# One fused kernel on one core: where the state's first expert products are kept between two steps, and when w2 is asked for

## The chip, the cores and the metric

The kernel runs on one core of a Trainium2 chip. The metric is device time in microseconds (us), as the median of several runs. TensorE (PE) does the matrix products, VectorE (DVE) and ScalarE (ACT) read its results out of PSUM, GpSimd (POOL) does some element-wise work, and SyncE (SP) issues most of the transfers (DMAs).

## The reference, cut to what matters

Three stages follow one another. `x` is (4, 8, 512, 64): 4 batches, 8 heads, 512 rows, 64 per head. `state` is (4, 8, 32, 64): 32 state slots per head.

```python
scores = scale * x @ state.T;   a  = softmax(scores);   xread = a @ state
scores2 = scale * state @ x.T;  a2 = softmax(scores2);  sread = a2 @ x
x1 = concat([xread, sread])                  # per batch 512 + 32 rows, 512 wide (8 heads x 64)
...
for e in range(8):                           # every token goes through every expert
    h = relu(x1 @ w1[e])                     # 512 -> 1024
    out += P[:, e:e + 1] * (h @ w2[e])       # 1024 -> 512
...
g = silu(out @ w_in); result = g @ w_out     # 512 -> 2048 -> 512
```

`P` is a softmax over the experts, balanced by 8 rounds of row and column sums. Since `xread = a @ state`, the product `xread @ w1[e]` equals `a @ (state @ w1[e])` head by head, and `state @ w1[e]` has only 32 rows per batch and head.

## The kernel before

All products are float32 made of three float32r products: each operand is split into a rounded high part and the rest, and `mm3` (L84 to L86) issues high x low, low x high, high x high. In this text `h_...` and `l_...` are the two parts of a weight, `hh` and `hl` those of the hidden values. `lo_of` (L89) writes a low part: source minus high part. The high part is a cast on ACT.

The second stage is bound to a list of steps. One expert is two **units** of 512 hidden columns, so there are 16 units `u`; a unit has 16 steps `k`, for batch b = k // 4 and hidden tile f = k % 4. Step i of the main loop issues on PE, in an order written out by hand: `S1` of the step two ahead (6 matmuls into `ph`, from the attention weights `aT` and `G[u, b]` = state @ w1), then `S2` of this step (12 matmuls into the four banks `po`, from `hh`, `hl` and the unit's w2), then small pieces. `S2`'s tile f of w2 is first needed at step k = f of its unit. ACT and DVE take `ph` to `hh` and `hl`. At the end of each batch four DVE operations add `po` to `acc` (L567). The order of the instructions on ACT, DVE, POOL and SP is made by a scheduler from the program's order; the order on PE is the program's.

`G` of unit u + 1 is made during unit u. `g_pair` is called inside `S2`, after its second tile, at steps 1 and 5 of most units (8 and 9 of unit 0, 8 and 10 of unit 1). It issues 12 products of half the contraction rows into four PSUM banks `pg`, two from the pool `p1` (2 banks, which `ph` uses too) and two from `pm` (2 banks, also for transposes and small results). For each bank ACT casts the high part, DVE makes the low part, both go into a tile `stg`, and a DMA writes it to DRAM (`g_d`). Four DMAs for each batch read it back (`load_g`, in the steps 8, 9, 11, 14), because a bank holds lanes (partitions) by batch and slot for one head, and `G` needs for one batch lanes by head and slot.

w1 and w2 come as raw tiles (`load_raw`, SP), which `load_split` casts on ACT and subtracts on DVE (on POOL in unit 0's w1). w2 of the next unit is asked for and cast at steps 12 to 15, behind `load_g` in the program, w1 of unit u + 2 at steps 7 to 10. At step 6 PE computes `psr` (the first product of the 32 x 4 `sread` rows; `sr_first`), and at step 7 `sread_second` adds their second product in a free `po` bank. The raw tiles share 3 buffers, the `stg` tiles 4.

Of the kernel before, what the change touches and what calls it, by code (L numbers as in the profile page):

```python
# [21 lines left out]
def fused_kernel(ctx: ExitStack, tc: tile.TileContext, x, state, w_gate, w1, w2, w_in, w_out, out):  # L22

# [79 lines left out]
    for b in range(B):  # L103
        nc.sync.dma_start(out=st[b * NS:(b + 1) * NS], in_=state[b].rearrange("h n d -> n h d"))
# [181 lines left out]
    def scores(b, rr, bank):  # L286
# [3 lines left out]
        for r in (2 * rr, 2 * rr + 1):  # L290
            for hp in range(KD):
# [3 lines left out]
                    bd[:, hp, bp, j ^ (hp & 1)].rearrange("p h n -> p (h n)"), start=True, stop=True,  # L295
# [33 lines left out]
    def positions(b, q):  # L329
# [4 lines left out]
        e2 = e2_of[b, q] = att.tile([128, 512], F32, tag="e2", name=f"e2_{b}_{q}", bufs=4)  # L334
# [91 lines left out]
    g_d = {}  # L426
# [4 lines left out]
    def g_pieces(u, hps, banks):  # L431
# [10 lines left out]
        for hp in hps:  # L442
            for half in range(2):
                ps = pg[hp, half]
                stg = stp.tile([128, 2, FU], F32R, tag="stg", name=f"stg{u}_{hp}_{half}")
                nc.scalar.copy(stg[:, 0], ps)
                lo_of(stg[:, 1], ps, stg[:, 0])
                nc.sync.dma_start(out=g_d[u][hp // 2, 2 * (hp & 1) + half], in_=stg.bitcast(F32))

    def g_first(bp, hp, bank=pm):  # L450
# [6 lines left out]
        halves = [(slice(64 * half, 64 * half + 64), 2 * bp + (half ^ (hp & 1))) for half in range(2)]  # L457
        for lanes, b in halves:
            nc.scalar.copy(G[0, b][lanes, hp // 2, 0], pg[lanes])
        for lanes, b in halves:  # L460
            lo_of(G[0, b][lanes, hp // 2, 1], pg[lanes], G[0, b][lanes, hp // 2, 0])

    def g_start(u):
        g_d[u] = dram.tile([2, 4, 128, 2, FU], F32, tag="g_d", name=f"g_d{u}", bufs=2)

    def g_pair(u, i):
        if i == 0:
            g_start(u)
        g_pieces(u, (2 * i, 2 * i + 1), (p1, pm))

    def load_g(u, b):
        g_tile(u, b)
# [5 lines left out]

    def sr_first(u):
# [22 lines left out]
    def S1(u, b, f):  # L502
# [11 lines left out]
        else:  # L514
# [88 lines left out]
    def both(piece, b, *bank):  # L603
# [165 lines left out]
```

## Time and profile before

| | |
|---|---|
| median of 3 runs | 1737.66 us (1737.47 to 1739.04) |
| profiled execution: its time, its span | 1744.39 us, 1742.6 us |
| TensorE's mean granted clock in it, share of full | 0.988 |
| PE, DVE, ACT, POOL busy in the span | 97%, 51%, 28%, 1% |
| DMA traffic in the span | 222.07 MB |

The span is the time from the first to the last instruction in the trace of one execution; its own time lies 6.7 us above the median of the runs, so a sum made on the span has to be set against that execution and then moved to the median. TensorE's share counts a matmul as busy from its start to its modelled end; neighbours overlap, so the start-to-start distance (0.227 us for a 512-column matmul at full clock) says more than the duration printed (0.39 us).

### The profile page before, as it was taken

To read this page: it belongs to the slowest core of one execution; us is meant where nothing else is said; L and a number is where in the kernel's file an instruction comes from. 1 tells how busy PE (TensorE), PEld (TensorE's weight loads), DVE (VectorE), ACT (ScalarE), POOL (GpSimd) and SP (SyncE) were. 2 spreads that over 40 slices of the span, in tenths; PEclk is the share of its full clock that TensorE was granted. 3 is DMA by queue.
4 is the path that set the end of the run, shared out by engine and by line. 5 is a ranking of instruction groups with operands and counts; after the bars stand their busy time and mean duration, and the time that the engine had idled before them with its cause. 6 is when DMAs were issued, how large, how long until landed. Compare 5 with 4: busy or idle time off the path is not lost.

```text
span 1742.6 us, 20238 instructions
## 1 busy us (share of the span) xinstructions
PE 1690.5 (97%) x7868; PEld 1396.2 (80%) x7868; DVE 891.2 (51%) x1524; ACT 492.3 (28%) x891; POOL 12.6 (1%) x15
## 2 busy tenths in 40 slices
PE   8999999999999999999999999999999999999999
PEld 7878787877878787878778787878788888888888
DVE  7642575555555555565655655465434433433333
ACT  5642244222222222232322222232212322222222
POOL 1010000000000000000000000000000000000000
PEclk9989999999999999999999999999999999999999
DMA  7042376565745464655647465655540103020211
GB/s 170 19 150 70 96 201 199 132 205 146 195 160 164 138 176 165 167 185 136 206 145 206 139 167 171 170 183 125 169 109 7 43 1 97 1 97 1 85 49 55
DMA packets 107631, 222.07 MB, mean 127 GB/s; under 512 B 28560, under 2 KB 44944, under 8 KB 107536
## 3 DMA queue, kind: packets, MB, share of 16 engines
q1 hardware_dynamic: 101152, 201.76, 40.5%
q10 hardware_dynamic: 6384, 19.02, 2.8%
q8 instruction: 62, 1.02, 0.2%
q14 instruction: 33, 0.27, 0.0%
HBM read 136.59 MB, written 84.15 MB: 127 GB/s over the span
## 4 chain that ended last, share of the span: by engine, by line
PE 79%; DVE 2%; issue 1%; ACT 1%; ACTq 0%; DVEq 0%
PE po L85 16%; PE po L84 15%; PE po L86 15%; PE ph L86 9%; PE ph L84 9%; PE ph L85 9%; PE pg L441 3%; DVE acc L567 1%; PE psr L85 1%; PE psr L84 1%; PE psr L86 1%; DVE l_w L89 1%; ACT hh L512 1%; PE px L591 0%; DVE hl L513 0%
## 5 line engine op out<-in xcount | busy, mean ns | idle before, releaser
L84 PE MATMUL po<-h_w,hl 128*128 128x512 f32 x1024 | 410.4, 401 | 22.7 <-ACT h_w L190 22.7
L85 PE MATMUL po<-l_w,hh 128*128 128x512 f32 x1024 | 406.6, 397 | 14.1 <-DVE l_w L89 14.1
L86 PE MATMUL po<-h_w,hh 128*128 128x512 f32 x1024 | 404.0, 395 | 0.0
L513 DVE SCALAR_TENSOR_TENSOR hl<-ph,hh 128x512 fp32r<-128x512 f32 x256 | 176.7, 690 | 419.8 <-ACT hh L512 419.3
L512 ACT ACTIVATE hh<-ph 128x512 fp32r<-128x512 f32 x256 | 153.2, 598 | 666.0 <-PE ph L86 662.2
L84 PEld LDWEIGHTS po<-h_w,hl 128*128 128x128 f32 x1024 | 194.7, 190 | 79.6 <-ACT h_w L190 29.8
L85 PEld LDWEIGHTS po<-l_w,hh 128*128 128x128 f32 x1024 | 195.0, 190 | 61.3 <-DVE l_w L89 22.5
L86 PEld LDWEIGHTS po<-h_w,hh 128*128 128x128 f32 x1024 | 195.1, 191 | 40.8
L84 PE MATMUL ph<-aTh,G 128*128 128x512 f32 x512 | 203.5, 398 | 0.4 <-DVE hl L513 0.4
L86 PE MATMUL ph<-aTh,G 128*128 128x512 f32 x512 | 200.2, 391 | 0.0
L85 PE MATMUL ph<-aTl,G 128*128 128x512 f32 x512 | 200.2, 391 | 0.0
L567 DVE SCALAR_TENSOR_TENSOR acc<-po,P,acc 128x512 f32<-128x512 f32 x224 | 153.1, 742 | 6.6 <-PE po L86 6.6
L523 DVE TENSOR_TENSOR gv<-ph,sg 128x384 f32<-128x384 f32 (+1 forms) x80 | 48.9, 611 | 191.2 <-ACT sg L521 191.2
L84 PE MATMUL ph<-x2h,wil 128*128 128x384 f32 (+1 forms) x320 | 115.4, 361 | 0.0
L86 PE MATMUL ph<-x2h,wih 128*128 128x384 f32 (+1 forms) x320 | 114.7, 358 | 0.0
L85 PE MATMUL ph<-x2l,wih 128*128 128x384 f32 (+1 forms) x320 | 114.4, 357 | 0.0
L86 PEld LDWEIGHTS ph<-aTh,G 128*128 128x128 f32 x512 | 96.5, 189 | 20.6
L84 PEld LDWEIGHTS ph<-aTh,G 128*128 128x128 f32 x512 | 96.9, 189 | 19.8 <-DVE hl L513 0.6
L85 PEld LDWEIGHTS ph<-aTl,G 128*128 128x128 f32 x512 | 96.8, 189 | 19.1
L86 PE MATMUL po<-woh,hh 128*128 128x512 f32 x272 | 106.8, 393 | 0.0
L85 PE MATMUL po<-wol,hh 128*128 128x512 f32 x272 | 106.7, 392 | 0.0
L84 PE MATMUL po<-woh,hl 128*128 128x512 f32 x272 | 105.8, 389 | 0.0
(163 smaller groups left out, 1848.9 us busy)
## 6 DMA issues: line engine op xcount, KB each, us to landing
g_d<-stg SPq DMA_DIRECT2D x120, 512.0 KB, 4.0
G<-g_d SPq DMA_DIRECT2D x240, 256.0 KB, 5.5
raw_w<-in_moe_w_dram SPq DMA_DIRECT2D x136, 256.0 KB, 5.3
raw<-in_moe_w_in_dram SPq DMA_DIRECT2D x16, 512.0 KB, 6.2
wi_d<-cvo ACTq DMA_DIRECT2D x16, 512.0 KB, 2.7
raw<-in_moe_w_out_dram SPq DMA_DIRECT2D x16, 512.0 KB, 6.3
wo_d<-cvo ACTq DMA_DIRECT2D x16, 512.0 KB, 3.1
x<-in_x_dram SPq DMA_DIRECT2D x16, 256.0 KB, 4.9
```

The costliest lines, as they stand in the source:

```text
L84: nc.tensor.matmul(ps, al, bh, start=first, stop=False)
L85: nc.tensor.matmul(ps, ah, bl, start=False, stop=False)
L86: nc.tensor.matmul(ps, ah, bh, start=False, stop=last)
L89: engine.tensor_tensor(out=lo, in0=src, in1=hi.bitcast(F32), op=ALU.subtract)
L441: nc.tensor.matmul(pg[hp, half], a[lanes[half], hp], w[lanes[half]], start=i == 0, stop=i == 2)
L512: nc.scalar.activation(out=hh, in_=ph, func=AF.Relu)
L513: last["dve"] = nc.vector.scalar_tensor_tensor(out=hl, in0=ph, scalar=0.0, in1=hh.bitcast(F32), op0=ALU.max, op1=ALU.subtract)
L523: nc.vector.tensor_tensor(out=gv[:, :n], in0=ph[:, :n], in1=sg[:, :n], op=ALU.mult)
L567: nc.vector.scalar_tensor_tensor(out=a, in0=ps, scalar=P[:, t, e:e + 1], in1=a, op0=ALU.mult, op1=ALU.add)
```

## The change

`state @ w1` no longer goes through DRAM. The (batch, head) pairs are placed so that every 32-lane quarter of a `pg` bank already stands on the lanes where its batch needs it (a Latin square over batch and head: `bd`, the attention scores' places and the reads of the slots follow the new placing). Each bank is copied, in float32, in four 32-lane pieces into one tile `g32`, two pieces by ACT and two by DVE in turn; `split_g` later makes the high part of one batch by an ACT cast of 128x1024 and the low part by a POOL subtraction, at steps 7, 8, 10, 14 (11 to 14 in units 0 and 1). `g_d` with its 360 transfers and the `stg` tiles go away. Raw w2 tiles are asked for at steps 10 (tile 0), 11 (tiles 1 and 2) and 12 (tile 3) for units from 1 on, with 4 raw buffers in place of 3; they are cast at steps 12 to 15 as before, now ahead of `split_g` in the program. At the start the state is loaded by eight transfers (four on SP, four on ACT) in place of four, its high and low part for `g_pair` are made by POOL from `bd`'s parts, the low parts of unit 1's w1 are also made on POOL, and `e2` has 3 buffers in place of 4. In step 2 of unit 0 `back(0)` stands ahead of `positions(1)`.

```diff
--- before
+++ after
...
     s8 = ctx.enter_context(tc.tile_pool(name="s8", bufs=8))
-    stp = ctx.enter_context(tc.tile_pool(name="stp", bufs=4))
+    gp = ctx.enter_context(tc.tile_pool(name="gp", bufs=1))
     accp = ctx.enter_context(tc.tile_pool(name="accp", bufs=4))
     wp = ctx.enter_context(tc.tile_pool(name="wp", bufs=5))
-    rawp = ctx.enter_context(tc.tile_pool(name="rawp", bufs=3))
+    rawp = ctx.enter_context(tc.tile_pool(name="rawp", bufs=4))
     hp_ = ctx.enter_context(tc.tile_pool(name="hp", bufs=4))
...
     st = att.tile([128, H, D], F32, tag="att", name="st")
-    for b in range(B):
-        nc.sync.dma_start(out=st[b * NS:(b + 1) * NS], in_=state[b].rearrange("h n d -> n h d"))
+    for p in range(2):
+        for b in range(B):
+            r, hs = NS * (b ^ p), slice(4 * p, 4 * p + 4)
+            (nc.scalar if p else nc.sync).dma_start(out=st[r:r + NS, hs], in_=state[b, hs].rearrange("h n d -> n h d"))
     x_sb = {}
...
     bd = const.tile([128, KD, 2, 2, 2, NS], F32, name="bd")
+    bdhl = gp.tile([128, 2, KD, 2, 2, 2, NS], F32R, tag="g32", name="bdhl")
+    bdh, bdl = bdhl[:, 0], bdhl[:, 1]
     sth = const.tile([128, KD, B * NS], F32R, name="sth")
...
         nc.tensor.transpose(pst4[:, hp].rearrange("p b n -> p (b n)"), st[:, 2 * hp:2 * hp + 2, :].rearrange("p h d -> p (h d)"), ident)
-    for hp in range(KD):
-        for j in range(2):
-            for half in range(2):
-                lanes = slice(64 * half, 64 * half + 64)
-                nc.vector.tensor_copy(
-                    bd[lanes, hp, :, j ^ (hp & 1), half, :],
-                    pst4[lanes, hp].rearrange("p (c j) n -> p c j n", j=2)[:, :, j, :],
-                )
+    for half in range(2):
+        lanes = slice(64 * half, 64 * half + 64)
+        for c in range(2):
+            nc.vector.tensor_copy(bd[lanes, :, c, :, half ^ c, :], pst4[lanes, :, 2 * c:2 * c + 2, :])
     flat = "p k c j h n -> p (k c j h n)"
-    bdh, bdl = (stp.tile([128, KD, 2, 2, 2, NS], F32R, tag="stg", name=f"bd{i}") for i in "hl")
     def split_state():
...
         lo_of(bdl.rearrange(flat), bd.rearrange(flat), bdh.rearrange(flat))
-        nc.scalar.copy(sth.rearrange("p k c -> p (k c)"), pst)
-        lo_of(stl.rearrange("p k c -> p (k c)"), pst, sth.rearrange("p k c -> p (k c)"))
+        for t, s in ((sth, bdh), (stl, bdl)):
+            v = s.bitcast(F32).rearrange("p k c j h n -> p k c (j h n)")
+            nc.gpsimd.tensor_tensor(out=t, in0=v[:, :, 0], in1=v[:, :, 1], op=ALU.add)
     def bd_of(t, hp, bp):
...
         else:
-            w1t[u, hp] = load_split(src, [128, FU], f"w1_{u}_{hp}", "w1", 4, nc.gpsimd if u == 0 else nc.vector)
-    def load_w2(u, f):
+            w1t[u, hp] = load_split(src, [128, FU], f"w1_{u}_{hp}", "w1", 4, nc.gpsimd if u <= 1 else nc.vector)
+    def load_w2(u, f, only_raw=False):
         e, fh = divmod(u, UPE)
         r0 = fh * FU + f * 128
-        w2t[u, f] = load_split(w2[e, r0:r0 + 128, :], [128, DM], f"w2_{u}_{f}", "w2", 5)
+        if only_raw:
+            load_raw(w2[e, r0:r0 + 128, :], [128, DM], f"w2_{u}_{f}")
+        else:
+            w2t[u, f] = load_split(w2[e, r0:r0 + 128, :], [128, DM], f"w2_{u}_{f}", "w2", 5)
...
             for half in range(2):
-                ps = pg[hp, half]
-                stg = stp.tile([128, 2, FU], F32R, tag="stg", name=f"stg{u}_{hp}_{half}")
-                nc.scalar.copy(stg[:, 0], ps)
-                lo_of(stg[:, 1], ps, stg[:, 0])
-                nc.sync.dma_start(out=g_d[u][hp // 2, 2 * (hp & 1) + half], in_=stg.bitcast(F32))
+                for i in range(4):
+                    to = (i // 2) ^ (hp // 2), half ^ (i & 1)
+                    r = slice(NS * i, NS * i + NS)
+                    dst = g32[u][r, 2 * to[1] + to[0], hp % 2]
+                    if i % 2 == half:
+                        nc.scalar.copy(dst, pg[hp, half][r])
+                    else:
+                        nc.vector.tensor_copy(dst, pg[hp, half][r])
     def g_first(bp, hp, bank=pm):
...
-    def g_start(u):
-        g_d[u] = dram.tile([2, 4, 128, 2, FU], F32, tag="g_d", name=f"g_d{u}", bufs=2)
+            lo_of(G[0, b][lanes, hp % 2, 1], pg[lanes], G[0, b][lanes, hp % 2, 0])
     def g_pair(u, i):
         if i == 0:
-            g_start(u)
+            g32[u] = gp.tile([128, B, 2, FU], F32, tag="g32", name=f"g32_{u}")
         g_pieces(u, (2 * i, 2 * i + 1), (p1, pm))
-    def load_g(u, b):
+    def split_g(u, b):
         g_tile(u, b)
-        for c in range(4):
-            r = NS * (c ^ (2 * (b & 1)))
-            nc.sync.dma_start(
-                out=G[u, b][r:r + NS].bitcast(F32), in_=g_d[u][:, c, b * NS:(b + 1) * NS].rearrange("q n w f -> n q w f")
-            )
+        src = g32[u][:, b]
+        nc.scalar.copy(G[u, b][:, :, 0], src)
+        lo_of(G[u, b][:, :, 1], src, G[u, b][:, :, 0], nc.gpsimd)
     def sr_first(u):
...
             mm3(ps, srh[:, hp], srl[:, hp], wh, wl, hp == 0, hp == KD - 1)
-        t = att.tile([128, FU], F32, tag="e2", name=f"hs_{u}", bufs=4)
+        t = att.tile([128, FU], F32, tag="e2", name=f"hs_{u}", bufs=3)
         nc.scalar.activation(out=t, in_=ps, func=AF.Relu)
...
         1: (both(positions, 0), [lambda hp=hp: x_turn(3, hp, pm) for hp in range(KD)]),
-        2: (both(positions, 1), both(back, 0) + both(scores, 3, pm) + [lambda: slots(3, 1), lambda: state_reads(0)]),
+        2: (both(back, 0), both(positions, 1) + both(scores, 3, pm) + [lambda: slots(3, 1), lambda: state_reads(0)]),
         3: (both(mixing, 2, pm), [lambda: g_first(1, 0)]),
...
                 convert_some((u - 2) * B * NF + k + 5)
+            if k >= 12:
+                load_w2(u + 1, k - 12) if u + 1 < NU else load_wout(0, k - 12)
             for unit, hp in first.get(u, {}).get(k, ()):
...
                 load_w1(u + 2, k - at)
-            loads = (12, 13, 14, 15) if u <= 1 else (8, 9, 11, 14)
+            for f in ({10: (0,), 11: (1, 2), 12: (3,)}.get(k, ()) if 1 <= u and u + 1 < NU else ()):
+                load_w2(u + 1, f, True)
+            loads = (11, 12, 13, 14) if u <= 1 else (7, 8, 10, 14)
             if u + 1 < NU and k in loads:
-                load_g(u + 1, loads.index(k))
-            if k >= 12:
-                load_w2(u + 1, k - 12) if u + 1 < NU else load_wout(0, k - 12)
+                split_g(u + 1, loads.index(k))
             if u == NU - 1:
```

How the change moves instructions, in unit 10 (in the names below the first number is the unit: `h_w2_10_2` is the high part of tile 2 of unit 10's w2, `stg11_0_1` the bank of head pair 0, half 1, of the next unit's G, `hh10_1_0` the hidden tile of batch 1, f = 0; the last number is a running one). On ACT before, around step 1 to 3:

```order
L512 ACTIVATE hh10_0_3_7333<-ph10_0_3_7326 128x512
L446 CAST stg11_0_0_7360<-pg11_0_0_7344 128x512
L446 CAST stg11_0_1_7364<-pg11_0_1_7345 128x512
L446 CAST stg11_1_0_7368<-pg11_1_0_7352 128x512
L446 CAST stg11_1_1_7372<-pg11_1_1_7353 128x512
L512 ACTIVATE hh10_1_0_7394<-ph10_1_0_7387 128x512
L190 CAST h_w2_10_2_7257<-raw_w2_10_2_7255 128x512
L190 CAST h_w2_10_3_7291<-raw_w2_10_3_7289 128x512
L512 ACTIVATE hh10_1_1_7418<-ph10_1_1_7411 128x512
```

The casts of w2's tiles 2 and 3 stand behind four `stg` casts and a `hh`. On ACT now, at the end of unit 9 and the first steps of unit 10:

```order
L195 CAST h_w2_10_2_7167<-raw_w2_10_2_7077 128x512
L519 ACTIVATE hh10_0_0_7149<-ph10_0_0_7142 128x512
L249 CAST cvo_21_7233<-cv_21_7073 128x512
L195 CAST h_w2_10_3_7202<-raw_w2_10_3_7112 128x512
L519 ACTIVATE hh10_0_1_7181<-ph10_0_1_7174 128x512
```

All four casts of unit 10's w2 (0 and 1 stand further up) are now ahead of `hh10_0_1`. Where the `stg` casts stood, ACT now has (with what each instruction waits for):

```order
L458 COPY g32_11_7254<-pg11_0_0_7255 32x512 [waits PE_49,Pool_49]
L458 COPY g32_11_7254<-pg11_0_1_7256 32x512 [waits DVE_49]
L458 COPY g32_11_7254<-pg11_1_0_7263 32x512 [waits PE_49]
L458 COPY g32_11_7254<-pg11_0_0_7255 32x512 [waits DVE_49]
L458 COPY g32_11_7254<-pg11_0_1_7256 32x512 [waits DVE_49]
L458 COPY g32_11_7254<-pg11_1_0_7263 32x512 [waits DVE_49]
L458 COPY g32_11_7254<-pg11_1_1_7264 32x512 [waits DVE_49]
L519 ACTIVATE hh10_1_0_7305<-ph10_1_0_7298 128x512 [waits PE_49]
L458 COPY g32_11_7254<-pg11_1_1_7264 32x512 [waits DVE_49]
L519 ACTIVATE hh10_1_1_7329<-ph10_1_1_7322 128x512 [waits PE_49,Activation_49]
```

Eight 32-lane copies stand in place of four casts, and six of them wait for a copy of the same bank on DVE; DVE has the other eight, which wait for ACT in the same way. The last copy of bank `pg11_0_1`, whose place in `p1` the next `ph` takes, is the fifth row. On DVE before, at steps 5 to 8, behind the four `stg` low parts of head pairs 2 and 3:

```order
L513 SCALAR_TENSOR_TENSOR hl10_2_0_7533<-ph10_2_0_7525,hh10_2_0_7532 128x512
L242 TENSOR_TENSOR cv_22_7385<-cv_22_7385,cvo_22_7563 128x512
L89 TENSOR_TENSOR l_w1_12_0_7616<-raw_w1_12_0_7613,h_w1_12_0_7615 128x512
L89 TENSOR_TENSOR l_w1_12_1_7650<-raw_w1_12_1_7647,h_w1_12_1_7649 128x512
L89 TENSOR_TENSOR l_w1_12_2_7695<-raw_w1_12_2_7692,h_w1_12_2_7694 128x512
L513 SCALAR_TENSOR_TENSOR hl10_2_1_7574<-ph10_2_1_7566,hh10_2_1_7573 128x512
L567 SCALAR_TENSOR_TENSOR acc1_1032<-po10_1_4_7451,P_172,acc1_1032 128x512
```

On DVE now, behind the eight copies of that place:

```order
L520 SCALAR_TENSOR_TENSOR hl10_2_0_7444<-ph10_2_0_7436,hh10_2_0_7443 128x512
L250 TENSOR_TENSOR cv_22_7296<-cv_22_7296,cvo_22_7474 128x512
L92 TENSOR_TENSOR l_w1_12_0_7527<-raw_w1_12_0_7524,h_w1_12_0_7526 128x512
L92 TENSOR_TENSOR l_w1_12_1_7564<-raw_w1_12_1_7561,h_w1_12_1_7563 128x512
L92 TENSOR_TENSOR l_w1_12_2_7607<-raw_w1_12_2_7604,h_w1_12_2_7606 128x512
L92 TENSOR_TENSOR l_w1_12_3_7637<-raw_w1_12_3_7634,h_w1_12_3_7636 128x512
L520 SCALAR_TENSOR_TENSOR hl10_2_1_7485<-ph10_2_1_7477,hh10_2_1_7484 128x512
L574 SCALAR_TENSOR_TENSOR acc1_1023<-po10_1_4_7362,P_163,acc1_1023 128x512
```

Four low parts of w1 instead of three stand ahead of `hl10_2_1` and the `acc1` rows (the fourth stood further down). POOL has these two rows in that stretch now, for the first two batches of unit 11's G (`split_g`):

```order
L92 TENSOR_TENSOR G_11_0_7530<-g32_11_7254,G_11_0_7530 128x2x512 [waits PE_49,Activation_49,Pool_49]
L92 TENSOR_TENSOR G_11_1_7567<-g32_11_7254,G_11_1_7567 128x2x512 [waits PE_49,Activation_49,Pool_49]
```

POOL, which had nothing here, now subtracts two tiles of 128x1024 in the same stretch. The rows of PE are the same products in the same order on both sides there.

## Rows read from the trace of the kernel before

**Rows 1.** Page, part 1: busy time, share of span, instructions of each engine.
```profile
PE 1690.5 (97%) x7868; PEld 1396.2 (80%) x7868; DVE 891.2 (51%) x1524; ACT 492.3 (28%) x891; POOL 12.6 (1%) x15
```

**Rows 2.** Waits of TensorE: releaser, us in total, times, longest us.
```profile
PE po L84 <- ACT h_w L190: 22.7, 17, 3.1
PE po L85 <- DVE l_w L89: 14.1, 22, 1.5
```

**Rows 3.** Timeline of TensorE: start, us, engine, line, operation, tiles [idle before].
```profile
832.01 0.39 PE L86 MATMUL ph<-aTh,G 128*128 128x512 f32 x1
833.65 0.49 PE L84 MATMUL po<-h_w,hl 128*128 128x512 f32 x1 [1.25 <-ACT h_w L190]
834.47 0.50 PE L85 MATMUL po<-l_w,hh 128*128 128x512 f32 x1 [0.32 <-DVE l_w L89]
```

**Rows 4.** Timeline of ScalarE over the same stretch.
```profile
828.57 2.06 ACT L446 CAST stg<-pg 128x512 fp32r<-128x512 f32 x4 [1.59 <-PE pg L441]
...
832.99 1.13 ACT L190 CAST h_w<-raw_w 128x512 fp32r<-128x512 f32 x2
```

**Rows 5.** Windows, ten units (5 to 14): length, busy times, granted clock, DMA share.
```profile
754.50:833.60 79.10, 77.49 (x340) 62.39 (x340) 42.28 (x68) 20.42 (x37) 0.00 (x0) 0.98 0.56 164
...
912.10:989.60 77.50, 75.91 (x341) 61.45 (x341) 45.50 (x76) 21.08 (x38) 0.00 (x0) 1.00 0.59 171
...
sum 791.00, PE 765.67 PEld 618.34 DVE 449.47 ACT 208.61 POOL 0.00; mean PE 76.57 PEld 61.83 DVE 44.95 ACT 20.86 POOL 0.00
```

**Rows 6.** Window behind the waits at the end of unit 8; columns as rows 5.
```profile
756.00:765.00 9.00, 9.00 (x38) 7.33 (x37) 3.69 (x7) 0.87 (x2) 0.00 (x0) 0.90 0.65 242
```

**Rows 7.** Timelines of TensorE, ScalarE and VectorE at step 5 of unit 10.
```profile
851.29 0.39 PE L84 MATMUL ph<-aTh,G 128*128 128x512 f32 x1
...
849.09 2.06 ACT L446 CAST stg<-pg 128x512 fp32r<-128x512 f32 x4 [1.65 <-PE pg L441]
...
849.71 2.48 DVE L89 TENSOR_TENSOR stg<-pg,stg 128x512 fp32r<-128x512 f32 x4 [1.22 <-ACT stg L446]
```

**Rows 8.** Groups by line and shape: ScalarE, VectorE, GpSimd (busy, mean ns).
```profile
L459 ACT CAST G<-pg 64x512 fp32r<-64x512 f32 x16 | 9.3, 580 | 1.5 <-PE pg L86 1.3
...
L143 ACT CAST bdh<-bd 128x1024 fp32r<-128x1024 f32 x1 | 1.1, 1056 | 0.0
...
L561 DVE COPY acc<-po 128x512 f32<-128x512 f32 x16 | 10.3, 682 | 0.0
...
L135 DVE COPY bd<-pst 64x64 f32<-64x64 f32 x16 | 3.6, 222 | 2.9 <-PE pst L130 2.7
...
L316 DVE TENSOR_TENSOR a<-a,z 128x512 f32<-128x512 f32 x2 | 1.4, 684 | 0.0
...
L89 POOL TENSOR_TENSOR l_w<-raw_w,h_w 128x512 fp32r<-128x512 f32 x8 | 11.0, 1389 | 108.2 <-ACT h_w L190 108.2
```

**Rows 9.** Timelines of VectorE and GpSimd where both work from SBUF.
```profile
16.73 1.78 DVE L309 TENSOR_TENSOR a<-s,m 128x512 f32<-128x512 f32 x1
...
16.68 2.96 POOL L89 TENSOR_TENSOR l_w<-raw_w,h_w 128x512 fp32r<-128x512 f32 x2 [0.50 <-ACT h_w L190]
...
119.44 0.83 DVE L89 TENSOR_TENSOR l_w<-raw_w,h_w 128x512 fp32r<-128x512 f32 x1
...
118.45 2.95 POOL L89 TENSOR_TENSOR l_w<-raw_w,h_w 128x512 fp32r<-128x512 f32 x2 [7.79 <-ACT h_w L190]
```

**Rows 10.** Timelines at steps 6 to 8 of unit 10: ScalarE, VectorE, TensorE.
```profile
856.25 1.98 ACT L190 CAST h_w<-raw_w 128x512 fp32r<-128x512 f32 x3 [2.80 <-PE psr L86]
...
856.91 2.05 DVE L89 TENSOR_TENSOR l_w<-raw_w,h_w 128x512 fp32r<-128x512 f32 x3 [1.94 <-ACT h_w L190]
...
860.95 2.72 DVE L567 SCALAR_TENSOR_TENSOR acc<-po,P,acc 128x512 f32<-128x512 f32 x4
...
862.17 0.39 PE L84 MATMUL po<-h_w,hsl 128*128 128x512 f32 x1
```

**Rows 11.** Timeline of TensorE in unit 0.
```profile
118.75 2.98 PE L361 MATMUL psr<-a2T,x 128*128 128x64 f32 x16 [1.62 <-DVE stg L89]
```

More of the change, by code (lines that the diff above doesn't have):

```diff
@@ L167, in gate_state @@
                 lanes = slice(64 * half, 64 * half + 64)
-                j = half ^ (hp & 1)
-                parts.append((pg4[lanes, hp], *(gg[lanes].rearrange("p (c j) q w e -> p c j q w e", j=2)[:, :, j, hp // 2, w, :] for w in range(2))))
+                j = half ^ (hp // 2)
+                parts.append((pg4[lanes, hp], *(gg[lanes].rearrange("p (c j) q w e -> p c j q w e", j=2)[:, :, j, hp % 2, w, :] for w in range(2))))
         for src, hi, lo in parts:
@@ L270, in x_turn @@
         if hp == 0:
-            place_of[b] = [2 * (k // 2) + ((k & 1) ^ (b % 2)) for k in range(KD)]
+            place_of[b] = [2 * (k % 2) + ((k // 2) ^ (b % 2)) for k in range(KD)]
             xT_of[b] = s8.tile([128, KD, R, 128], F32, tag="s8", name=f"xT{b}")
@@ L294, in scores @@
                     pl[:, c0:c0 + 64], xT_of[b][:, hp, r, :],
-                    bd[:, hp, bp, j ^ (hp & 1)].rearrange("p h n -> p (h n)"), start=True, stop=True,
+                    bd[:, hp, bp, j ^ (hp // 2)].rearrange("p h n -> p (h n)"), start=True, stop=True,
                 )
@@ L333, in positions @@
             nc.tensor.transpose(pq[:, r * 128:(r + 1) * 128], s1_of[b][:, r, q * 128:(q + 1) * 128], ident)
-        e2 = e2_of[b, q] = att.tile([128, 512], F32, tag="e2", name=f"e2_{b}_{q}", bufs=4)
+        e2 = e2_of[b, q] = att.tile([128, 512], F32, tag="e2", name=f"e2_{b}_{q}", bufs=3)
         nc.scalar.copy(e2, pq)
@@ L364, in state_reads @@
             lanes = slice(64 * half, 64 * half + 64)
-            parts.append((psr4[lanes, :, half * NS:(half + 1) * NS], *(t[lanes, :, b * NS:(b + 1) * NS] for t in (srh, srl))))
+            cb = half ^ (b // 2)
+            parts.append((psr4[lanes, :, cb * NS:(cb + 1) * NS], *(t[lanes, :, b * NS:(b + 1) * NS] for t in (srh, srl))))
         for src, hi, lo in parts:
@@ L424, in fused_kernel @@
     s2p = {}
-    g_d = {}
+    g32 = {}
     def g_tile(u, b):
@@ L456, in g_first @@
         mm3(pg, bd_of(bdh, hp, bp), bd_of(bdl, hp, bp), *w1t[0, hp], True, True)
-        halves = [(slice(64 * half, 64 * half + 64), 2 * bp + (half ^ (hp & 1))) for half in range(2)]
+        halves = [(slice(64 * half, 64 * half + 64), 2 * bp + (half ^ (hp // 2))) for half in range(2)]
         for lanes, b in halves:
-            nc.scalar.copy(G[0, b][lanes, hp // 2, 0], pg[lanes])
+            nc.scalar.copy(G[0, b][lanes, hp % 2, 0], pg[lanes])
         for lanes, b in halves:
-            lo_of(G[0, b][lanes, hp // 2, 1], pg[lanes], G[0, b][lanes, hp // 2, 0])
-    def g_start(u):
-        g_d[u] = dram.tile([2, 4, 128, 2, FU], F32, tag="g_d", name=f"g_d{u}", bufs=2)
+            lo_of(G[0, b][lanes, hp % 2, 1], pg[lanes], G[0, b][lanes, hp % 2, 0])
     def g_pair(u, i):
         if i == 0:
-            g_start(u)
+            g32[u] = gp.tile([128, B, 2, FU], F32, tag="g32", name=f"g32_{u}")
         g_pieces(u, (2 * i, 2 * i + 1), (p1, pm))
-    def load_g(u, b):
+    def split_g(u, b):
         g_tile(u, b)
-        for c in range(4):
-            r = NS * (c ^ (2 * (b & 1)))
-            nc.sync.dma_start(
-                out=G[u, b][r:r + NS].bitcast(F32), in_=g_d[u][:, c, b * NS:(b + 1) * NS].rearrange("q n w f -> n q w f")
-            )
+        src = g32[u][:, b]
+        nc.scalar.copy(G[u, b][:, :, 0], src)
+        lo_of(G[u, b][:, :, 1], src, G[u, b][:, :, 0], nc.gpsimd)
     def sr_first(u):
@@ L519, in S1 @@
                 mm3(ph[:, :n], wh[:, k], wl[:, k], xh, xl, k == 0, k == KD - 1)
-            sg = att.tile([128, 512], F32, tag="e2", name=f"sg{u}_{b}_{f}", bufs=4)
+            sg = att.tile([128, 512], F32, tag="e2", name=f"sg{u}_{b}_{f}", bufs=3)
             nc.scalar.activation(out=sg[:, :n], in_=ph[:, :n], func=AF.Sigmoid)
```

## Prediction

> **What bounds the kernel now.** I read four things, in this order. First the busy shares: TensorE is busy 97% of the span, the other engines half or less [rows 1], so the time is TensorE's own work plus its gaps, and DMA traffic counts only where TensorE waits for it. Second, what TensorE waits for: two lines hold 36.8 us in 39 waits (22.7 and 14.1), the high and the low part of w2 [rows 2]. Third, one such place in order of time. At 833.65 TensorE has waited 1.25 us for the cast of w2's third tile and then 0.32 us for its low part [rows 3]; on ScalarE that cast begins at 832.99, and ahead of it stand four `stg` casts that began at 828.57 and a `hh` [rows 4]. The reader is to see that the raw tile is not what is late: the cast is, behind work for the next unit's G. Fourth, windows: ten units take 791.0 us, 79.1 each [rows 5].
>
> **What the waits cost.** The idle time understates it, since matmuls overlap. From 832.01 to 833.65 are 1.64 us, against a pitch of 0.227: 1.41 lost for 1.25 of idle; from 833.65 to 834.47 it is 0.82, so 0.59 lost for 0.32, part of it the restart. I add 0.27 us per wait as in the second case (0.16 as in the first): 36.8 + 39 x 0.27 = 47 us (43 to 47). Behind some of the longest waits the granted clock also falls: 0.90 of full over the 9 us from 756 to 765 [rows 6], and 0.98 over the 79.1 us of the unit with that stretch [rows 5]. In such a stretch TensorE runs in part at 1.2 in place of 2.4 GHz, and a stretch at that level costs half its length; what is lost to it is one less the clock, times the length, 79.1 x 0.02 = 1.6 us here, and over units 1 to 15 I estimate 10 us, from six such units. So 57 us hang on the late w2. A unit of 77.5 us with 2.3 us of such losses in it gives 75.2 us without [rows 5].
>
> **What the change removes.** In the new order all four casts of a unit's w2 stand ahead of its second `hh`, each held only until TensorE frees its slot, which happens before the `hh` beside it is due. So I take all 57 us off. The 360 transfers through DRAM cost only queue time on SP, hidden behind TensorE, and I price them at nothing; the cover is the slack of two or more steps between a batch's G and its first use.
>
> **What it adds: the copies.** At step 5 of unit 10 the `stg` casts begin at 849.09 and the next `ph` comes at 851.29, 2.20 us later; it needs the bank free, and the two passes of 4 (2.06 us on ScalarE, 2.48 us on VectorE) let it go in time [rows 7]. Now each bank is emptied by four copies in turn on two engines. Half the lanes take no less time: a 64-lane cast is 580 ns, as long as a quarter of the 2.06 us [rows 7, 8]. So a 32-lane copy is 0.60 us on ScalarE and 0.68 on VectorE (682 for a full one [rows 8]; the floor would be the 222 ns of a 64-lane copy of 64 columns [rows 8], but that has an eighth of the columns). Chained with the handoffs, ScalarE's last copy of the bank that `ph` takes is its fifth: it starts at 2.27 and ends at 2.87, so `ph` at 2.92 in place of 2.20: 0.72 us at step 5, 0.65 at step 1, and 0.11 for each restart. From 0 (floor) to 1.2 (each handoff 0.05 more), I take it as worked.
>
> **What it adds: the low parts on GpSimd.** The last copy ends 5.8 us after the start; ScalarE's two 128x1024 casts (1056 ns [rows 8]) follow to 7.85; GpSimd's subtractions, 2 x 1.28 us each by an undisturbed 128x512 one (the mean of 1389 has the disturbed ones in it [rows 8]), run from 6.95 to 9.5 and on to about 12.7. In the same stretch VectorE has four `l_w1` with two inputs in SBUF, ready from about 8.65, and behind them `hl` and the accumulations whose first must end before `sread_second` can start. Before, that first accumulation ended about 861.70, a quarter of the 2.72 us behind 860.95, and `sread_second` ran at 862.17: slack 0.47 [rows 10]. What happens when both engines read SBUF is seen twice in this trace. At 16.73 VectorE's subtraction took 1.78 us beside GpSimd's 16.68 one, where the like of it (L316) takes 684 ns [rows 8, 9]: a loss of 1.09. At 119.44 an `l_w` beside GpSimd's 118.45 pair took 0.83 [rows 9], a loss of 0.15. Four times the second is 0.6 us, which the slack takes and nothing is lost; four times the first, 4.4, is more than GpSimd's own work there. Taking turns, four `l_w` of 0.68 end at about 14.5, `hl` at 15.1, the first accumulation at 15.86; `sread_second` comes at 15.95, where 13.8 would have been its time: 2.15 us, and a restart. I take this, nearest to the first row, bounds 0 and 3.7.
>
> The Trainium skill says in "SBUF — State Buffer", "Who interferes with whom", that a VectorE instruction with two SBUF inputs and a GpSimd instruction that reads SBUF share a port under an exclusive lock, and that whichever comes second blocks for the whole of the first. By that rule the sum has the 2.15 us; by the 0.83 us row alone it has none. The 1.78 us row agrees with the rule; the 0.83 us row, near the end of GpSimd's work, does not exclude it.
>
> **The sum.** Per unit 0.72 + 0.65 + 2.15 + 3 restarts = 3.85 us in eleven units (2 to 13 but 7, whose second GpSimd tile comes behind two `l_w1`); 75.2 + 3.85 = 79.05, against 79.1 before: there the change is a wash. Units 7 and 14 pay 1.5 each. Together 42.4 + 3 = 45 us. Units 0 and 1 have the pairs at steps 8 and 9, 8 and 10, where transposes and `psr` take the banks of `pm` right behind: there TensorE waits already 1.62 us for `stg` [rows 11], and the banks come free 2 to 3 us later now; per pair 2.5 to 3 us, 10 us in all (4 to 15). The start, with weight casts that wait for transfers ahead of `xT` and the state's parts on GpSimd, 1.5 us (0 to 3). The 2-us waits are of the size behind which the clock fell before in about a third of the cases; an estimate of 5 us (0 to 18: eleven times the 1.6 above). The moved `back(0)` and the smaller `e2` pool cost nothing: ScalarE and VectorE have two steps of room there; without it, under 1 us, once. Sum: -57 + 45 + 10 + 1.5 + 5 = +4.5 on the span of 1742.6. That execution's own time of 1744.39 is 6.7 above the median of 1737.66, so on the median's scale 1737.7 + 4.5 = **1742 us**.
>
> **The rivals.** (B) *The lock costs nothing*: VectorE's slowdown is as at 119.44. The eleven waits of 2.26 go (25 us), and the clock's 5: 1712 us. For it: one of two rows; against: the other, and the rule. (C) *The clock pays*: every `sread` wait is followed by a half-level stretch as at 756; 18 in place of 5, 1755 us, slower; it decides from about half of the units on. Against it: most 1.25-us waits had none behind them. (D) *The change doesn't do what it says*: a w2 cast, held by its slot, holds the `hh` behind it on ScalarE's queue, so a wait of 1 us returns in 15 units; 1757 us. Against: the slot is freed a step ahead. (E) *The copies are short*: if 32 lanes take nearer 0.25 us, the pairs' waits go (20 us) and GpSimd is done before the `l_w1` are ready; 1742 - 20 - 30 = 1692. Only the 64-column row speaks for it.
>
> **How the numbers follow.** Two times within 0.2% (3.5 us) can't be told apart here: 1734.2 to 1741.1 is "same". Chances: the forecast 0.53, its own range 1732 to 1752; B 0.25; C 0.13; D 0.04; E 0.05. The range goes from B to C and D, 1712 to 1757, which leaves E and the outer parts of C out. Faster: B, E, and 0.07 of the forecast: 0.37. Same: 0.22 of the forecast. Slower: its other 0.24, C and D: 0.41.
>
> **What would show it.** Right: no waits for `h_w` or `l_w` in TensorE's list at `po`; new ones at `ph` for a copy, some 0.5 us each (the idle shows less than is lost), and at `sread_second`'s `po` for an accumulation, near 2 us in eleven units; GpSimd's subtractions near 2.56 us with `l_w1` beside them well above 0.69. Wrong: `l_w1` at 0.69 to 0.85 beside GpSimd (B), a granted clock under 0.98 in most units (C), `h_w` waits left (D), copies under 0.4 us (E). The sum fails most easily at the lock, which decides 25 us, and at units 0 and 1, which are bounded from few rows.

## The result, and the profile after

The changed kernel takes 1757.91 us, median of 4 runs (1756.99 to 1761.19), beside 1738.35 us for the kernel before (1737.47 to 1742.43): ratio 1.0111, 95% interval 1.009 to 1.0133, so it is slower by 0.9 to 1.3%. The profiled execution has a span of 1756.6 us (own time 1758.68); that of before had 1742.6 (1744.39). The forecast was 1742 us with a range to 1757.

The busy line of the page, which answers to [rows 1]:

```profile
PE 1683.4 (96%) x7868; PEld 1392.0 (79%) x7868; DVE 1036.0 (59%) x1623; ACT 631.5 (36%) x1070; POOL 176.1 (10%) x85
```

TensorE has 7 us less busy time in a span 14 us longer: it waits more. Its waits, longest groups, which answer to [rows 2] (releaser, us in total, times, longest us):

```profile
PE ph L87 <- issue: 27.5, 25, 1.8
PE po L87 <- DVE acc L574: 15.1, 11, 1.6
PE psr L369 <- DVE g L460: 5.3, 1, 5.3
PE pt L359 <- ACT g L458: 3.7, 1, 3.7
PE pl L301 <- ACT xT L292: 2.9, 2, 2.7
```

Not one wait on `h_w` or `l_w` at `po` is left. In their place stand 25 waits at `ph` of 1.1 us each (the view names no releaser for them, "issue"; the first product of the next `ph` needs a bank that `g_pair` has filled, and in the run with w1's low parts on GpSimd below 15 of these waits are put down to ScalarE's copy), eleven at `po` for an accumulation, 1.4 us each, and single long ones in unit 0 (`psr`, `pt`) and at the start (`pl`). The units, by windows (the same columns as [rows 5]); the sum is over six of them at full clock, five of 79.3 to 79.5 us and one, unit 7, of 77.8:

```profile
759.80:839.20 79.40, 76.02 (x340) 61.34 (x341) 53.14 (x82) 29.66 (x49) 10.12 (x4) 1.00 0.21 67
...
sum 474.90, PE 455.63 PEld 368.06 DVE 332.48 ACT 180.12 POOL 61.14; mean PE 75.94 PEld 61.34 DVE 55.41 ACT 30.02 POOL 10.19
```

One unit in order of time. TensorE, then ScalarE, VectorE, GpSimd; they answer to [rows 7, 10]:

```profile
938.13 0.47 PE L87 MATMUL ph<-aTh,G 128*128 128x512 f32 x1 [0.95 <-issue]
950.76 0.50 PE L87 MATMUL po<-h_w,hsl 128*128 128x512 f32 x1 [1.49 <-DVE acc L574]
...
934.74 0.58 ACT L458 COPY g<-pg 32x512 f32<-32x512 f32 x1 [1.59 <-PE pg L450]
935.65 2.99 ACT L458 COPY g<-pg 32x512 f32<-32x512 f32 x5 [0.33 <-DVE g L460]
...
943.85 5.60 DVE L92 TENSOR_TENSOR l_w<-raw_w,h_w 128x512 fp32r<-128x512 f32 x4 [1.89 <-ACT h_w L195]
...
949.98 0.73 DVE L574 SCALAR_TENSOR_TENSOR acc<-po,P,acc 128x512 f32<-128x512 f32 x1
...
942.48 5.22 POOL L92 TENSOR_TENSOR G<-g,G 128x1024 fp32r<-128x1024 f32 x2 [41.62 <-ACT G L483]
```

`ph` starts at 938.13, when ScalarE's fifth copy of the pair is out: the first begins at 934.74 and the other four, with one more, run from 935.65 in turns with VectorE. From the first copy to `ph` are 3.39 us, where 2.20 were before. Later GpSimd's two subtractions hold 942.48 to 947.70, and VectorE's four `l_w` need 5.60 us from 943.85 (2.49 at the same place in the run with GpSimd idle, below); the accumulation at 949.98 is what `po` waits for until 950.76.

### The profile page after: what moved, and what is told of

Its sections match the earlier page's. It is cut to its first block, busy times and chain, and to the rows that moved or that the text cites. A ratio compares the mean times of both kernels' runs of the same rounds, so it can differ in the third digit from the quotient of the medians.

```text
span 1756.6 us, 19915 instructions
## 1 busy us (share of the span) xinstructions
PE 1683.4 (96%) x7868; PEld 1392.0 (79%) x7868; DVE 1036.0 (59%) x1623; ACT 631.5 (36%) x1070; POOL 176.1 (10%) x85
## 4 chain that ended last, share of the span: by engine, by line
PE 88%; DVE 7%; issue 3%; ACT 2%; DMA 1%; SPq 0%; POOL 0%; ACTq 0%; DVEq 0%
PE po L87 17%; PE po L89 16%; PE po L88 16%; PE ph L87 10%; PE ph L89 10%; PE ph L88 10%; PE pg L450 2%; DVE l_w L92 2%; DVE g L460 1%; PE psr L369 1%; PE pl L301 1%; PE psr L89 1%; PE psr L88 1%; PE psr L87 1%; DVE hl L520 1%
## 5 line engine op out<-in xcount | busy, mean ns | idle before, releaser
L87 PE MATMUL po<-h_w,hl 128*128 128x512 f32 x1024 | 404.3, 395 | 0.0
L89 PE MATMUL po<-h_w,hh 128*128 128x512 f32 x1024 | 399.0, 390 | 0.0
L88 PE MATMUL po<-l_w,hh 128*128 128x512 f32 x1024 | 398.8, 389 | 0.0
L92 POOL TENSOR_TENSOR G<-g,G 128x1024 fp32r<-128x1024 f32 x60 | 150.8, 2523 | 1001.8 <-ACT G L483 850.2
L460 DVE COPY g<-pg 32x512 f32<-32x512 f32 x240 | 164.7, 687 | 19.0 <-PE pg L450 12.4
L458 ACT COPY g<-pg 32x512 f32<-32x512 f32 x240 | 138.6, 578 | 78.3 <-PE pg L450 42.6
L92 DVE TENSOR_TENSOR l_w<-raw_w,h_w 128x512 fp32r<-128x512 f32 x120 | 118.9, 1014 | 64.5 <-ACT h_w L195 64.2
L87 PEld LDWEIGHTS ph<-aTh,G 128*128 128x128 f32 x512 | 96.7, 189 | 61.1 <-issue 38.8
L528 ACT ACTIVATE sg<-ph 128x384 f32<-128x384 f32 (+1 forms) x80 | 42.8, 535 | 220.0 <-PE ph L89 220.0
```

Source lines behind the costliest of these rows:

```text
L87: nc.tensor.matmul(ps, al, bh, start=first, stop=False)
L88: nc.tensor.matmul(ps, ah, bl, start=False, stop=False)
L89: nc.tensor.matmul(ps, ah, bh, start=False, stop=last)
L92: engine.tensor_tensor(out=lo, in0=src, in1=hi.bitcast(F32), op=ALU.subtract)
L458: nc.scalar.copy(dst, pg[hp, half][r])
L460: nc.vector.tensor_copy(dst, pg[hp, half][r])
```

## The experiments

Each ratio is to the kernel before, run beside it on the same chip; differences to the changed kernel are between medians unless a span is named.

**The kernel before, once more** (no edit).

> The kernel before, unchanged, profiled a second time. Theory: the 10 us that the forecast took off for the half-level clock belong to that one execution, whose own time lies 6.7 us above the median; another execution near 1738 us has fewer such stretches (less than 12 us at half level after 200 us, where there were 20.5) and the same 39 waits of about 37 us on h_w and l_w at po. Rival: the stretches are the kernel's own, then they come again with some 20 us, and the offset lies elsewhere.

It took 1740.2 us with a span of 1738.4. Its waits on w2, and the granted clock (third last number) in two windows:

```profile
PE po L84 <- ACT h_w L190: 22.6, 17, 3.1
PE po L85 <- DVE l_w L89: 14.1, 22, 1.5
...
100.00:146.00 46.00, 43.75 (x230) 36.67 (x229) 17.64 (x42) 18.50 (x45) 5.52 (x4) 0.85 0.66 189
752.00:761.00 9.00, 9.00 (x37) 7.36 (x37) 3.81 (x7) 0.99 (x2) 0.00 (x0) 0.90 0.66 244
```

The first of these windows in the first profile of before (the second one is [rows 6], 4 us later in that execution):

```profile
100.00:146.00 46.00, 43.59 (x216) 36.31 (x216) 16.38 (x40) 17.44 (x42) 5.51 (x4) 0.78 0.66 189
```

The rival holds for the long part: the stretch at 752 us, like three others after 200 us, is there again with the same clock. The 4.2 us between the two spans lie in the first 200 us: 46 us at 0.78 in place of 0.85 are 3.2 of them. Over all runs of before that were made beside the experiments it took 1734.98 to 1746.36 us.

**Low parts of `split_g` on VectorE.**

```diff
-        lo_of(G[u, b][:, :, 1], src, G[u, b][:, :, 0], nc.gpsimd)
+        lo_of(G[u, b][:, :, 1], src, G[u, b][:, :, 0])
```

> The changed kernel with split_g's low parts on VectorE in place of GpSimd, nothing else. Theory (the two engines lock each other out when both read SBUF): with GpSimd idle there, the l_w of w1 take 0.69 us in place of 1.4, the eleven waits of 1.5 us for the accumulation go or fall under 0.4 us, although VectorE has two subtractions of 1.2 us more in the same stretch: about 1740 us, 18 under the changed kernel. Rival (VectorE simply has too much work or gets the casts too late): 2.4 us more work in that stretch make each wait longer by about 2 us: about 1780 us.

1739.07 us, ratio 0.9994 (0.9979 to 1.0009). No wait for an accumulation is left. In the changed kernel the `l_w` on VectorE, GpSimd's subtractions and the 32-lane copies take (groups by line and shape, mean ns behind the comma):

```profile
L460 DVE COPY g<-pg 32x512 f32<-32x512 f32 x240 | 164.7, 687 | 19.0 <-PE pg L450 12.4
...
L92 POOL TENSOR_TENSOR G<-g,G 128x1024 fp32r<-128x1024 f32 x60 | 150.8, 2523 | 1001.8 <-ACT G L483 850.2 <-PE po L89 70.9 <-DVE cv L239 26.5
L458 ACT COPY g<-pg 32x512 f32<-32x512 f32 x240 | 138.6, 578 | 78.3 <-PE pg L450 42.6 <-DVE g L460 31.9
L92 DVE TENSOR_TENSOR l_w<-raw_w,h_w 128x512 fp32r<-128x512 f32 x120 | 118.9, 1014 | 64.5 <-ACT h_w L195 64.2
```

In this one the `l_w`, and the work that was added to VectorE:

```profile
L92 DVE TENSOR_TENSOR l_w<-raw_w,h_w 128x512 fp32r<-128x512 f32 x120 | 79.8, 687 | 42.9 <-ACT h_w L195 42.9
L92 DVE TENSOR_TENSOR G<-g,G 128x1024 fp32r<-128x1024 f32 x60 | 72.4, 1221 | 6.9 <-ACT G L483 6.9
```

VectorE does 72.4 us more, and its `l_w` are 327 ns shorter in the mean. It was not short of time; GpSimd's subtractions held it up.

**Low parts of w1 on GpSimd**, the mirror.

```diff
-"w1", 4, nc.gpsimd if u <= 1 else nc.vector)
+"w1", 4, nc.gpsimd)
```

> The changed kernel with the low parts of w1 on GpSimd in all units, next to split_g's. The mirror of the run with split_g on VectorE: that one emptied GpSimd, this one takes the two-input work from SBUF off VectorE. Theory (the lock): hl and the accumulation of batch 1 no longer stand behind a locked l_w, the eleven waits of 1.5 us go, 18 us less, about 1740 us, though GpSimd is busy twice as long; what VectorE does beside it with two inputs in SBUF (the weight conversion) gets slower and nobody waits for it. Rival (GpSimd's work is late for TensorE in itself): waits for l_w or G appear, 1755 us or more.

1740.83 us, ratio 1.0012 (1.0 to 1.0023). The accumulation waits are gone and those at `ph` stay, though GpSimd has 56 subtractions more than in the changed kernel:

```profile
PE ph L87 <- ACT g L458: 16.3, 15, 1.6
PE ph L87 <- issue: 12.9, 12, 1.8
...
L92 POOL TENSOR_TENSOR l_w<-raw_w,h_w 128x512 fp32r<-128x512 f32 x72 | 96.9, 1372 | 140.3 <-ACT h_w L195 131.2 <-DMA raw_w<-in_moe_w_dram 9.0
```

So either engine may have the work, but not both at once: the same conclusion from the other side.

**One engine for each bank.**

```diff
-                    if i % 2 == half:
+                    if half == 1:
                         nc.scalar.copy(dst, pg[hp, half][r])
```

> The changed kernel with each PSUM bank emptied by one engine (half 1 by ScalarE, half 0 by VectorE), as many copies as before on each engine. Theory (the turn-taking chain in a bank holds the next ph): ScalarE's four copies of the bank that ph takes end some 2.3 us after the start, the 26 waits of 1 us at ph in units 2 to 14 go to 0.3 us or less, 20 to 30 us less; GpSimd starts earlier too, which takes something off the accumulation waits: 1715 to 1735 us. Rival (the number of copies, not their turn-taking): waits as long as before, 1755 to 1760 us.

1739.41 us, ratio 0.999 (0.9977 to 1.0004). Waits, then the pair's eight copies on ScalarE and the next `ph`:

```profile
PE po L87 <- DVE acc L574: 17.7, 12, 1.9
PE ph L87 <- issue: 6.0, 22, 1.0
...
919.39 4.72 ACT L458 COPY g<-pg 32x512 f32<-32x512 f32 x8 [1.78 <-PE pg L450]
...
921.83 0.47 PE L87 MATMUL ph<-aTh,G 128*128 128x512 f32 x1 [0.19 <-issue]
```

The 22 waits at `ph` are 0.27 us each now, and the kernel is 18.5 us faster than the changed one, where 20 to 30 were expected. The number of copies is the same, and so, nearly, is their pitch: 0.59 us, and 0.60 in turns. What the turns cost is the order. The bank that `ph` takes is empty after ScalarE's fourth copy in place of its fifth, and the idle 0.33 us behind the first copy, a wait for VectorE's copy, is gone: `ph` comes 2.44 us after the first copy in place of 3.39. The waits for the accumulation did not shrink (17.7 us in place of 15.1): that part of the expectation failed. GpSimd starts earlier, but TensorE arrives earlier too.

**All state loads on SP's queue.**

```diff
-            (nc.scalar if p else nc.sync).dma_start(out=st[r:r + NS, hs], ...
+            nc.sync.dma_start(out=st[r:r + NS, hs], ...
```

> The changed kernel with all eight state loads on SP's queue. On ScalarE two xT copies then stand ahead of the w1 casts again, one cast between them. Theory (the start's loss is this order, with a clock that falls behind it): the waits of 2.7 and 0.9 us at pl go, pl starts near 12.5 in place of 14.15, the half-level stretch from about 14.5 to 24.7 goes, 3 to 6 us less: about 1753 us. Rival (the start is late for another reason, such as the state's parts on GpSimd): no change, 1757 us, or later x tiles make it worse.

1753.42 us, ratio 1.0066 (1.0051 to 1.0081), span 1751.4. The 2.7 us wait at `pl` is gone. Only the queue of the loads was changed, and with it the scheduler put the first `xT` ahead of the w1 casts again, which wait for transfers. `pl` starts at 13.48 and not near 12.5 as expected, so most of the 5.2 us between the spans is clock: 1.00 in the window from 14 to 26 us, where the changed kernel has 0.57, against 0.88 in place of 1.00 in the 14 us before.

```profile
14.00:26.00 12.00, 11.09 (x83) 9.86 (x83) 9.77 (x17) 10.00 (x18) 6.14 (x5) 1.00 1.11 224
```

**The three together.**

> The changed kernel with three of its costs taken away together: low parts of split_g on VectorE, each bank emptied by one engine, state loads on SP. Theory (three separate causes): the gains of the single runs add up, 19 + 18.5 + 4.5 us: about 1716 us, 1710 to 1722, with under 10 us left of waits at ph and none for the accumulation. Rival (they share a cause, the late banks): about 1735 us.

1710.85 us, ratio 0.9832 (0.9812 to 0.9851). By spans, the three single kernels are 19.5, 22.6 and 5.2 us under the changed one (1737.1, 1734.0 and 1751.4 against 1756.6), 47.3 in all, which would give 1709.3; this one has 1707.3. By medians the single gains are 18.8, 18.5 and 4.5 us, 41.8 in all, and the three together gain 47.1. So they are separate causes whose gains add up, by medians with 5 us more than the sum, which no run explains. No wait for the accumulation is left, and under 7 us of waits at `ph`.

**Only the early requests for w2, in the kernel before.** G goes through DRAM as it did.

```diff
+            for f in ({10: (0,), 11: (1, 2), 12: (3,)}.get(k, ()) if 1 <= u and u + 1 < NU else ()):
+                load_w2(u + 1, f, True)      # load_raw alone; load_split finds it at steps 12 to 15
             loads = (12, 13, 14, 15) if u <= 1 else (8, 9, 11, 14)
```

> The kernel before with nothing but w2's raw tiles asked for at steps 10 (tile 0), 11 (1 and 2) and 12 (3); G still goes through DRAM, 3 raw buffers. Theory (the gain of the change is the order of w2's casts on ScalarE, and its cost is the on-chip G): all four casts stand ahead of the stg casts here too, the 39 waits go, and nothing of the new cost comes: 45 to 57 us under the kernel before, about 1690 us. Rival (the waits go only because G's transfers left SP's queue): the raw tiles land late behind them, hh waits behind casts that wait for a transfer, and at most 15 us are won: 1725 us or more.

1687.7 us, ratio 0.9705 (0.9679 to 0.973), 70 us under the changed kernel. What is left of the waits on w2 (all in unit 1; 0.6 us more are for `l_w`), and five units in windows, 75.13 us each:

```profile
PE po L84 <- ACT h_w L190: 2.3, 2, 1.2
...
sum 375.63, PE 375.63 PEld 307.58 DVE 226.60 ACT 104.96 POOL 0.00; mean PE 75.13 PEld 61.52 DVE 45.32 ACT 20.99 POOL 0.00
```

TensorE is busy in all of each unit. What gains is the request and the order of the casts that comes with it; the rest of the change was not needed.

**The changed kernel without the early requests.**

```diff
-            for f in ({10: (0,), 11: (1, 2), 12: (3,)}.get(k, ()) if 1 <= u and u + 1 < NU else ()):
-                load_w2(u + 1, f, True)
```

> The changed kernel with w2's raw tiles asked for where they are cast, at steps 12 to 15 as before the change. Theory (without G's transfers on SP's queue the order of the casts is right even so): the casts stand in the same places on ScalarE, no wait on h_w or l_w comes back, same time as the changed kernel within 0.3%. Rival (the early request is what removes the waits): h_w waits of 20 us or more come back, 1780 us or more.

1764.7 us, ratio 1.0144 (1.0121 to 1.0167), 0.3% above the changed kernel by the ratios, with intervals that overlap. The waits at `ph` (27.4 us) and for the accumulation (14.5) are those of the changed kernel. No wait on `h_w` or `l_w` came back; 3.1 us of the difference are one wait at `pc` (5.1 us in place of 2.0 for two). Either part of the change removes the waits on w2, and the on-chip G is the part that costs.

**The early requests in unit 0 as well.**

```diff
-...if 1 <= u and u + 1 < NU else ()):
+...if u + 1 < NU else ()):
```

> The kernel before with the early w2 requests in unit 0 as well, so for unit 1's w2 too. Theory: the last two pairs of waits on w2 (2.3 and 0.6 us of idle, at 178 and 187 us) go, 4 us less than with requests from unit 1 on: about 1683.5 us. Rival: in unit 0 the raw buffers are taken by w1 then, the casts come no earlier: 1687 us.

1682.29 us, ratio 0.9677 (0.9654 to 0.97), the fastest kernel here. The last waits on w2 are gone from TensorE's list. In time the 4 us expected are not shown, since its interval overlaps with that of the run with requests from unit 1 on. In the traces they are: from the first `sread` product of unit 0 to that of unit 1 are 41.16 us here and 44.84 there.

## Why the prediction was wrong

The four mechanisms were in their places, and the kernel became slower, which the forecast had as the likelier way by a little (0.41 against 0.37 for faster). Two terms of the sum were priced too low: the waits for the copies, and the start with units 0 and 1. Two others were priced too high and hid a part of that.

The terms come apart against the kernel with the early requests alone, which has none of the new cost. The first `S2` product of units 0, 1, 2 and 15, of the changed kernel:

```profile
46.48 0.48 PE L87 MATMUL po<-h_w,hl 128*128 128x512 f32 x1
186.50 0.40 PE L87 MATMUL po<-h_w,hl 128*128 128x512 f32 x1
273.54 0.39 PE L87 MATMUL po<-h_w,hl 128*128 128x512 f32 x1
1305.02 0.39 PE L87 MATMUL po<-h_w,hl 128*128 128x512 f32 x1
```

and of the kernel with the early requests alone:

```profile
41.27 0.48 PE L84 MATMUL po<-h_w,hl 128*128 128x512 f32 x1
168.65 0.40 PE L84 MATMUL po<-h_w,hl 128*128 128x512 f32 x1
253.60 0.39 PE L84 MATMUL po<-h_w,hl 128*128 128x512 f32 x1
1231.71 0.39 PE L84 MATMUL po<-h_w,hl 128*128 128x512 f32 x1
```

The changed kernel is 5.2 us behind when unit 0 begins, 17.9 at unit 1, 19.9 at unit 2 and 73.3 at unit 15. Inside unit 10, the first `S2` product of steps 1, 2, 7 and 8, in the same order:

```profile
912.74 0.39 PE L87 MATMUL po<-h_w,hl 128*128 128x512 f32 x1
920.05 0.39 PE L87 MATMUL po<-h_w,hl 128*128 128x512 f32 x1
946.40 0.39 PE L87 MATMUL po<-h_w,hl 128*128 128x512 f32 x1
954.98 0.39 PE L87 MATMUL po<-h_w,hl 128*128 128x512 f32 x1
```

```profile
860.17 0.39 PE L84 MATMUL po<-h_w,hl 128*128 128x512 f32 x1
866.19 0.39 PE L84 MATMUL po<-h_w,hl 128*128 128x512 f32 x1
891.24 0.39 PE L84 MATMUL po<-h_w,hl 128*128 128x512 f32 x1
898.04 0.39 PE L84 MATMUL po<-h_w,hl 128*128 128x512 f32 x1
```

From step 1 to 2, where the first `g_pair` stands, the changed kernel takes 7.31 us and the other 6.02: 1.29 lost. The second pair, at step 5, loses 1.30 in the same way, and `sread_second`, between steps 7 and 8, loses 1.78 (8.58 against 6.80). Summed over the units by the same differences:

| term, us | forecast | measured |
|---|---|---|
| the start | 1.5 | 5.2 |
| units 0 and 1 | 10 | 14.7 |
| waits for the copies, units 2 to 14 | 20.5 | 34.9 |
| waits for the accumulation, eleven units | 24.9 | 18.4 |
| clock behind these waits | 5 | 0 |

*What bounds the kernel, what the change removes: right.* 57 us were taken off for the late w2. The early requests alone, which do just that, have a span of 1683.5, 59 us under the first profile of before and 55 under the second, and a unit without losses is 75.13 us where 75.2 was worked out.

*The first step that failed: the price of the copies, 14 us.* The mechanism was right. With the restarts a unit was to lose 1.59 us at its two pairs and loses 2.6. The fifth copy on ScalarE was to start 2.27 us after the first; it started 2.7 after, because the second came 0.91 after the first (0.33 of it a wait for VectorE's copy) and the others follow 0.60 apart. So `ph` came 3.39 us after the first copy at step 5, and not 2.92.

*The lock on SBUF: right, its price some 6 us too high.* The instructions one by one, VectorE's first two `l_w` and GpSimd's two subtractions:

```profile
943.85 1.58 DVE L92 TENSOR_TENSOR l_w<-raw_w,h_w 128x512 fp32r<-128x512 f32 x1 [1.89 <-ACT h_w L195]
945.36 2.89 DVE L92 TENSOR_TENSOR l_w<-raw_w,h_w 128x512 fp32r<-128x512 f32 x1
...
942.48 2.41 POOL L92 TENSOR_TENSOR G<-g,G 128x1024 fp32r<-128x1024 f32 x1 [41.62 <-ACT G L483]
944.84 2.86 POOL L92 TENSOR_TENSOR G<-g,G 128x1024 fp32r<-128x1024 f32 x1
```

Each `l_w` ends 0.55 us after the subtraction that had begun before it, and GpSimd's second subtraction is 0.45 us longer than its first, as with strict turns. The rule of the Trainium skill ("SBUF — State Buffer", "Who interferes with whom"), an exclusive lock, gives this behaviour. In the two runs that moved the work to one engine, either way, the wait for the accumulation is gone. Of the two rows of before, the 1.78 us one [rows 9] was the one to go by. The 0.83 us one does not speak against the lock: taken singly, GpSimd's first subtraction there ended at 119.72, 0.28 us after the `l_w` had begun, and its second took 1.72 us in place of 1.27.

The first accumulation was to end 15.86 us after the first copy; it ended at 949.98 + 0.73 - 934.74 = 15.97. That it fits so well is in part luck: GpSimd began 0.8 us later than worked out (7.74 against 6.95 after the first copy), and its subtraction takes 2.41 us and not 2.56. TensorE loses 1.78 us there and not 2.26, because it comes later itself, after its longer waits for the copies. So the two errors hid each other: 79.4 us in the unit shown, forecast 79.05.

*The second step that failed: the start and units 0 and 1, 20 us where 11.5 stood.* The order at the start (w1's casts, which wait for transfers, ahead of `xT`) was named in the forecast and priced at 1.5 us with nothing behind it. What that price left out is the clock behind the wait. Windows of the changed kernel (granted clock third last), behind `pl` and around `pt` and `psr` of unit 0:

```profile
14.00:26.00 12.00, 10.97 (x45) 10.00 (x46) 6.32 (x8) 4.42 (x9) 5.51 (x4) 0.57 1.27 256
100.00:146.00 46.00, 36.34 (x180) 30.00 (x179) 25.45 (x56) 27.78 (x57) 10.90 (x7) 0.81 0.12 41
```

and the same ones of the kernel with the early requests alone:

```profile
14.00:26.00 12.00, 10.47 (x64) 8.91 (x64) 10.98 (x18) 9.53 (x18) 4.25 (x3) 0.86 1.18 244
100.00:146.00 46.00, 43.69 (x244) 36.70 (x244) 17.78 (x42) 18.54 (x44) 5.53 (x4) 0.93 0.66 189
```

At 0.57 in place of 0.86 over 12 us, the first costs 3.5 us, and the state loads on SP alone give back 5.2 us of the span. Unit 0 is 12.6 us longer. TensorE waits 3.7 us at `pt` and 5.3 at `psr`, where the other kernel waits 1.6 in all: 7.4 us more. The other 5 or so are clock, 0.81 against 0.93 over 46 us, and they are not shown to come from the change: the kernel before has 0.78 and 0.85 in that window in its two executions, and the execution compared with has the highest of these. In unit 1 the changed kernel pays two waits of 1.3 us at `ph` and 2.0 at `pc`, 6.2 us in all by the starts of the steps, and saves 4.1 on unit 1's w2, which the other still waits for.

*The clock.* The 5 us that the sum had for it were meant for the waits of units 2 to 13, and there it stayed at 1.00.

*The sum against the median.* The sum gave +4.5 us on the span; it is +14.0: 59.1 off for the early requests, 19.9 on up to unit 2, 53.4 in units 2 to 14, and -0.2 behind them. The 6.7 us between the first execution of before and the median were then taken as fixed. They belong in part to that execution: the second profile of before is 4.2 us shorter, most of it by the clock in its first 200 us. On medians the change costs 19.6 us. So of the miss of 16, some 10 are the sum and 6 the base.

*The rivals.* B and C did not happen: the lock cost 18.4 us, and the clock stayed at 1.00. D did not: no `h_w` wait came back. E did not: the 32-lane copies take 578 and 687 ns, as long as full ones. That C and D had 1755 and 1757 us, near the measured time, is chance.

## What to carry to other kernels

When an operand is late, look first at what stands ahead of its cast in the engine's queue: asking for the raw tile earlier moved the cast in the scheduler's order and won 3%, while the rebuilt path won nothing that the request had not won. Two engines that take turns on PSUM banks let the first bank go only after pieces of the others have been copied; give each engine its own bank. Before work goes to GpSimd, look whether VectorE has two-input work from SBUF at that moment, and price a wait at the start of a kernel with the clock that may fall behind it. Check the terms of a sum one by one even where the sum fits: here one price that was too low and one that was too high hid each other in every unit.

## What the runs showed of the hardware that I had not expected

Two waits of about 1 us in each unit of the changed kernel, and in eleven of them one of 1.5 us more, left the granted clock at 1.00 in all of units 2 to 14, while the kernel before had stretches at half level (1.2 of 2.4 GHz) at the same four places after 200 us in both executions, each behind waits on w2. In the first 200 us two executions of one kernel differ in it (0.78 and 0.85 in the window from 100 to 146 us), and with it in time.
